# Local-attention scores by 64-column products over both heads, and one 128-column product for a unit's last slot logits

## The chip, the cores and the metric

The program runs on one core of a Trainium2 chip, in one launch. The metric is device time in microseconds, the median of several runs. Engines: TensorE (PE; its weight loads are listed apart as PEld), VectorE (DVE), ScalarE (ACT), GpSimd (POOL) and SyncE (SP), which issues nearly all DMAs here.

## What is computed

An attention layer (batch 4, 8 heads, 576 tokens, head size 64) and two mixture-of-experts layers after it. The change is in the attention's local branch and in the slot logits of the first mixture (a soft one).

```python
q_d, k_d, v_d = (mean over groups of 4 tokens of q, k, v)
out_up = repeat(softmax(q_d @ k_d.T / 8) @ v_d, 4)
mask = abs(pos[:, None] - pos[None, :]) < 4
scores = where(mask, q @ k.T / 8, -1e9)
out_local = softmax(scores) @ v
x = (out_up + out_local)           # (2304, 512) after the heads are joined
logits = x @ phi                   # (2304, 32), 8 experts of 4 slots
d = softmax(logits, axis=0); c = softmax(logits, axis=1)
x = c @ experts(d.T @ x)           # soft mixture
out = top-2 mixture of x           # second mixture, 8 experts
```

## The kernel before

**Units and blocks.** The attention goes over 16 units, each one batch and a pair of heads; the two heads' 64 dimensions fill the 128 partitions. A unit's 576 tokens are cut into 10 groups of 58, each of two halves of 29 (`HQ`); a half needs 35 keys (`KW`). `K` holds the keys [128 dims of both heads, tokens]. `Q` is [128, head, token]: for head h only that head's 64 partitions are filled and the others are zero, so that a product over all 128 partitions gives that head's scores alone.

**Local scores.** `b_s` (line 275) first writes the mask into a PSUM tile by one bf16 product (line 277) and then adds the scores: for 10 groups, 2 halves and 2 heads one product of 32 query columns as weights by 35 keys (line 283), 40 in a unit. Each of the 40 writes 32 of the 128 partitions, in the order half, head, query.

**Soft part and transposes.** `soft_m` to `soft_l2` (lines 295 to 318) make the softmax on DVE and ACT, `soft_p` (line 320) scales the rows on POOL into `P`, and one step later `c_p` (line 361) transposes `P` into `PT`. `d_pe` (line 396) multiplies by the values: 20 products of 64 weight columns by 58 columns of `PT`, each on one quarter of the array (line 405).

**Slot logits.** Two steps later `logit_pe` (line 450) multiplies the unit's output, transposed (`xT`), by `phi_sb`: four products of 32 weight columns by 128 tokens (line 454), and for the last 64 tokens the same product four times, once into each quarter of the partitions (line 457), because `logit_add` (line 461) adds and the slot softmax reads all 128 partitions.

**Order.** The order is written out by hand. In each of the 16 steps a loop (line 577) goes over the table `SEQ` (line 19), and each entry issues one function for the unit of its offset (line 537): `S` is `b_s` of unit p, `CP` and `CD` the transposes of unit p-1, `A0` and `A1` the transposes that bring in keys and queries of unit p+1 (`a_pe`, line 218), `DP` and `DD` the products by values of unit p-1, `EP` and `LG` the transposes and logits of unit p-2. Every engine takes its instructions in that order. After the last step `TSEQ` (line 21) orders the tail.

**Bringing in K and Q.** `a_evac` (line 228) copies the transposed keys and queries out of PSUM, even and odd tokens apart: of a unit's 8 copies ACT makes 6 and DVE 2 (DVE makes the four of `Q` for unit 0). `Q`'s copies write every second element. `a_dve` and `a_pool` (lines 234, 245) sum groups of four tokens on DVE and POOL.

**DMA.** SP issues loads of keys, queries and values for coming units, zero fills of outputs, and the first mixture's weights, in the order of `SEQ`; eight DMAs are in flight at most. When the attention's memory is given back (`ring_2`, line 613) more weights follow. The first mixture, the routing of the second and its expert loop (line 1238 on) come after that.

Of the kernel before, what the change touches and what calls it, by code (L numbers as in the profile page):

```python
# [7 lines left out]
F32 = mybir.dt.float32  # L8
# [4 lines left out]
ALU = mybir.AluOpType  # L13
# [23 lines left out]
def attn_moe_moe_kernel(ctx: ExitStack, tc: tile.TileContext, q, k, v, moe_phi, moe_w1, moe_w2,  # L37
                        w_gate, w_noise, noise, w1, w2, out, dbg=None):
    nc = tc.nc
    B, H, S, D = q.shape  # L40
# [4 lines left out]
    NS = moe_phi.shape[1]  # L45
# [5 lines left out]
    HQ = 29  # L51
    KW = HQ + 6
# [35 lines left out]

    phi_sb = const.tile([128, 4, NS], F32, name="phi_sb")
    wgn = const.tile([128, 4, 2 * E], F32, name="wgn")  # L90
# [17 lines left out]
    with ExitStack() as tctx:  # L108
# [18 lines left out]
        mask = a1.tile([128, NG, KW], BF, name="mask")  # L127
        for a in range(4):
            nc.gpsimd.iota(dk[32 * a:32 * a + 32], pattern=[[1, KW]], base=0, channel_multiplier=-1,
                           allow_small_or_imprecise_dtypes=True)  # L130
        nc.vector.tensor_scalar(mtmp[:, 0], dk, 0.0, -1e9, op0=ALU.is_lt, op1=ALU.mult)
        nc.vector.tensor_scalar(mtmp[:, 1], dk, 6.0, -1e9, op0=ALU.is_gt, op1=ALU.mult)
        nc.vector.tensor_tensor(mtmp[:, 0], mtmp[:, 0], mtmp[:, 1], op=ALU.add)
# [23 lines left out]
        K = a1.tile([128, 592], F32, name="K")  # L157
        Q = a1.tile([128, 2, 592], F32, name="Q")
        Dq = a1.tile([128, 3, 2, 48], F32, name="Dq")
# [6 lines left out]
        for h in range(2):  # L166
            nc.vector.memset(Q[64 * h:64 * h + 64, 1 - h], 0.0)
            nc.vector.memset(Q[64 * h:64 * h + 64, h, S:592], 0.0)

# [58 lines left out]
        def a_evac(u, i, h, r):  # L228
            hs = slice(64 * h, 64 * h + 64)
            dst = Q[hs, h, 0:576] if i else K[hs, 3:579]  # L230
            cp(f"a{i}{h}{r}", dst.rearrange("p (m r) -> p r m", r=2)[:, r], AT[u, i, h][64 * r:64 * r + 64, 0:288],
               u == 0 and i == 1)

        def a_dve(u, h):
            hs = slice(64 * h, 64 * h + 64)
            if h:
                return nc.vector.tensor_reduce(out=Dq[hs, :, h], in_=Q[hs, h, 0:576].rearrange(
                    "p (a n r) -> p a n r", a=3, r=4), axis=AX.X, op=ALU.add)
            q4 = Q[hs, h, 0:576].rearrange("p (n r) -> p n r", r=4)
            q2 = wka.tile([128, 512], F32, name="s2", bufs=1)[hs, 0:288].rearrange("p (n r) -> p n r", r=2)  # L240
            nc.gpsimd.tensor_tensor(q2, q4[:, :, 0:2], q4[:, :, 2:4], op=ALU.add)
            q2 = q2.rearrange("p (a n) r -> p a n r", a=3)
            nc.gpsimd.tensor_tensor(Dq[hs, :, h], q2[:, :, :, 0], q2[:, :, :, 1], op=ALU.add)
# [31 lines left out]
        def b_s(u):  # L275
            s = ps.tile([128, 512], F32, name="S")
            nc.tensor.matmul(s[:, 0:NG * KW], idb, mask.rearrange("p g k -> p (g k)"), start=True, stop=True)
            for g in range(NG):
                for a in range(2):
                    for h in range(2):  # L280
                        p0 = 64 * a + 32 * h
                        c0 = 58 * g + HQ * a
                        nc.tensor.matmul(s[p0:p0 + 32, KW * g:KW * g + KW], Q[:, h, c0:c0 + 32], K[:, c0:c0 + KW],  # L283
                                         start=False, stop=True, skip_group_check=True)
            SS[u] = s
# [110 lines left out]
        def d_pe(u):  # L396
            b, hp = units[u]
            V = Vs[u % 2]
            xl = XL[u]
            PTv = PT.rearrange("p j g (a h i) -> p j g h a i", a=2, h=2)  # L400
            for j in range(5):
                for g in range(2):
                    gs = slice(64 * g, 64 * g + 64)
                    for h in range(2):
                        nc.tensor.matmul(xl[64 * h:64 * h + 64, g, 58 * j:58 * j + 58], V[gs, j, h],  # L405
                                         PTv[gs, j, g, h, :, 0:HQ], start=True, stop=True, skip_group_check=True)
# [43 lines left out]
        def logit_pe(u, t2=None):  # L450
            xT, kk = XT[u], u % 4
            L = (ET_[u][1] if t2 is None else t2)[:, 128:320]
            for t in range(4):
                nc.tensor.matmul(L[32 * t:32 * t + 32, 0:128], phi_sb[:, kk], xT[:, 128 * t:128 * t + 128],
                                 start=True, stop=True, skip_group_check=True)
            for t in range(4):
                nc.tensor.matmul(L[32 * t:32 * t + 32, 128:192], phi_sb[:, kk], xT[:, 512:576], start=True,
                                 stop=True, skip_group_check=True)
            LL[u] = L
# [117 lines left out]
        for p in range(-1, NU - 1):  # L577
            if p == 0:
                nc.sync.dma_start(out=phi_sb, in_=moe_phi.rearrange("(k p) s -> p k s", p=128))
            if p >= 5 and small:  # L580
# [509 lines left out]
    with ExitStack() as gctx:  # L1090
# [94 lines left out]
        for i in range(NTILE - 1):  # L1185
            n = NTILE - 1 - i
# [204 lines left out]
```

## Time and profile before

| | |
|---|---|
| median of 3 runs | 514.81 us (514.27 to 521.28) |
| profiled execution | 511.0 us, of it span 509.2 us |
| attention, from the second unit's step to the last (S of unit 2 to S of unit 15) | 26.7 to 149.2 us of the span |
| first mixture | about 169 to 210 us |
| second mixture | 210 us to the end |
| PE busy | 465.7 us, 91% |
| PE instructions recorded | 5257 products and 5257 weight loads |

Times in the views are microseconds from the start of the span unless marked ns. A 32-bit product is recorded twice (line 283: 640 products in the program, 1280 records), each time with a weight load of its own; a transpose is recorded once. Products are pipelined, so the length of one (some 0.2 us) is much more than the distance to the next. In `128*32 128x35`, 128*32 are the rows and columns of the array that the product takes, and 35 the columns that stream through. "Issue" is idle time in which an engine waited for nothing that the profile shows.

### The profile page before, as it was taken

The page shows a single profiled execution, that of the slowest core. Times are in us where ns is not written, and L with a number is a line of the kernel's source. Part 1 is how long each engine was busy: PE and PEld are TensorE (multiplying, and loading weights), DVE is VectorE, ACT ScalarE, POOL GpSimd, SP SyncE. Part 2 cuts the span into 40 slices and gives each one's busy share as a digit, 9 for nine tenths or more (in the row PEclk, how much of TensorE's full clock was granted, in tenths as well). Part 3 has the DMA queues.
Part 4 walks back from the last instruction along what each step waited for, and adds up shares of the span by engine and source line. Part 5 has one row for each costly group of instructions (what it writes and reads, how often), then busy time and mean ns, then how long its engine had stood idle before and what let it go on. Part 6 is the DMA issues. An engine that isn't in the chain of part 4 may idle for free.

```text
span 509.2 us, 13403 instructions
## 1 busy us (share of the span) xinstructions
PE 465.7 (91%) x5257; PEld 352.8 (69%) x5257; DVE 280.0 (55%) x717; ACT 277.8 (55%) x712; POOL 194.9 (38%) x291
## 2 busy tenths in 40 slices
PE   5798998999798999799969979999999999999993
PEld 4676777767575443477757758788787887878882
DVE  7787888888785321896538226166362552634400
ACT  2778678868676012554238157384662755636410
POOL 5655445535431101076566851232122222222222
PEclk9799899999999999869988989999999999999998
DMA  8999999989957999963373369796856857333333
GB/s 207 280 265 308 256 250 283 244 248 338 262 165 244 397 391 399 396 233 124 118 154 66 65 186 364 207 325 135 237 125 156 265 95 198 41 43 41 41 43 44
DMA packets 74668, 104.90 MB, mean 206 GB/s; under 512 B 30826, under 2 KB 40810, under 8 KB 74602
## 3 DMA queue, kind: packets, MB, share of 16 engines
q1 hardware_dynamic: 67690, 91.15, 55.4%
q0 software_dynamic: 6912, 12.85, 17.1%
q8 instruction: 43, 0.70, 0.6%
q14 instruction: 23, 0.19, 0.1%
HBM read 83.92 MB, written 20.05 MB: 204 GB/s over the span
## 4 chain that ended last, share of the span: by engine, by line
PE 58%; issue 18%; DMA 9%; ACT 5%; DVE 4%; POOL 2%; POOLq 2%; SPq 1%; ACTq 0%
PE y L1044 27%; DMA wr<-in_moe_w_dram 5%; PE S L283 3%; PE xl L412 2%; PE t L224 2%; DMA ld<-in_q_dram 2%; PE Sd L291 2%; PE gx L859 2%; PE hp L785 2%; PE xl L405 2%; PE gx L1024 1%; PE t L366 1%; POOL out_dram L1063 1%; ACT K L212 1%; PE yacc L807 1%
## 5 line engine op out<-in xcount | busy, mean ns | idle before, releaser
L1044 PE MATMUL y<-whi,hl 128*128 128x512 f32 x320 | 129.0, 403 | 0.0
L1044 PE MATMUL y<-whi,hh 128*128 128x512 f32 x320 | 128.6, 402 | 0.3 <-ACT hh L1025 0.3
L1044 PE MATMUL y<-wlo,hh 128*128 128x512 f32 x320 | 128.8, 402 | 0.0
L1063 POOL DMA_INDIRECT out_dram<-ys,idx x40 | 63.4, 1585 | 118.9 <-ACT ys L1050 67.6
L1050 ACT ACTIVATE ys<-y,gt 128x512 f32<-128x512 f32 x40 | 27.5, 687 | 84.5 <-issue 39.9
L1016 DVE TENSOR_TENSOR wlo<-wr,whi 128x512 fp32r<-128x512 f32 x64 | 42.2, 697 | 54.9 <-ACT whi L1013 54.3
L1044 PEld LDWEIGHTS y<-wlo,hh 128*128 128x128 f32 x320 | 61.4, 192 | 14.2 <-issue 1.4
L1044 PEld LDWEIGHTS y<-whi,hl 128*128 128x128 f32 x320 | 61.5, 192 | 11.9 <-issue 2.0
L1044 PEld LDWEIGHTS y<-whi,hh 128*128 128x128 f32 x320 | 61.3, 192 | 12.0 <-ACT hh L1025 0.6
L1026 DVE SCALAR_TENSOR_TENSOR hl<-h,hh 128x256 fp32r<-128x256 f32 (+1 forms) x64 | 31.4, 490 | 32.2 <-ACT hh L1025 30.7
L324 POOL TENSOR_TENSOR P<-El,su 64x350 f32<-64x350 f32 x31 | 24.0, 773 | 65.1 <-DVE su L317 42.8
L988 POOL DMA_INDIRECT tab<-stk,pos x36 | 36.6, 1016 | 16.4 <-issue 15.8
L1025 ACT ACTIVATE hh<-h 128x256 fp32r<-128x256 f32 (+1 forms) x64 | 28.0, 437 | 17.4 <-PE h L1024 12.9
L1013 ACT ACTIVATE whi<-wr 128x512 fp32r<-128x512 f32 x64 | 37.1, 626 | 0.2
L1026 DVE SCALAR_TENSOR_TENSOR hl<-gx,hh 128x256 fp32r<-128x256 f32 (+1 forms) x64 | 31.3, 489 | 9.1 <-ACT hh L1025 7.0
L1025 ACT ACTIVATE hh<-gx 128x256 fp32r<-128x256 f32 (+1 forms) x64 | 28.1, 439 | 14.1 <-PE gx L1024 11.3
L1062 POOL MEMSET spacer<- 1x1 f32 x40 | 18.0, 451 | 39.6 <-issue 39.6
L212 ACT ACTIVATE K<-t 64x288 f32<-64x288 f32 x64 | 27.7, 433 | 5.0 <-PE t L224 3.5
L212 ACT ACTIVATE PT<-t 64x256 f32<-64x256 f32 (+1 forms) x50 | 20.7, 417 | 14.9 <-PE t L366 14.2
L224 PE MATMUL t<-idf,ld 96*128 96x96 f32 x192 | 23.1, 274 | 5.5 <-DMA ld<-in_k_dram 4.3
L224 PEld LDWEIGHTS t<-idf,ld 96*128 96x128 f32 x192 | 19.4, 157 | 9.4 <-DVE on__133 L147 4.3
L875 DVE TENSOR_TENSOR GS<-gx,ghi 32x256 fp32r<-32x256 f32 x28 | 11.7, 419 | 24.1 <-ACT ghi L869 23.6
(297 smaller groups left out, 821.6 us busy)
## 6 DMA issues: line engine op xcount, KB each, us to landing
wr<-in_moe_w_dram SPq DMA_DIRECT2D x120, 256.0 KB
wr<-in_moe_w_dram SPq DMA_DIRECT2D x56, 512.0 KB
out_dram<-zero SPq DMA_DIRECT2D x20, 256.0 KB
V<-in_v_dram SPq DMA_DIRECT2D x62, 80.0 KB
ld<-in_k_dram SPq DMA_DIRECT2D x16, 288.0 KB
ld<-in_q_dram SPq DMA_DIRECT2D x16, 288.0 KB
XT<-tab SPq DMA_DIRECT2D x6, 320.0 KB
tab<-zero SPq DMA_DIRECT2D x7, 256.0 KB
```

The source lines that it names most:

```text
L212: nc.scalar.activation(dst, src, AF.Copy)
L224: nc.tensor.transpose(t[:, c:288:3], ld[:, i, h, 128 * c:128 * c + 128], idf[0:96, 0:96])
L324: eng.tensor_tensor(P[as_, :, HQ * a:HQ * a + KW], El[as_], su[as_, :, None].to_broadcast([64, NG, KW]), op=ALU.mult)
L988: st = nc.gpsimd.indirect_dma_start(out=tab, out_offset=bass.IndirectOffsetOnAxis(ap=pos[:, c, i:i + 1], axis=0), in_=stk[:, i].bitcast(F3 ...
L1013: nc.scalar.activation(whi[:, kk], wb(kk), AF.Copy)
L1016: eng.tensor_tensor(wlo[:, kk], wb(kk), whi[:, kk].bitcast(F32), op=ALU.subtract)
L1025: nc.scalar.activation(hh[:, f], h, AF.Relu)
L1026: nc.vector.scalar_tensor_tensor(hl[:, f], h, 0.0, hh[:, f].bitcast(F32), op0=ALU.max, op1=ALU.subtract)
L1044: nc.tensor.matmul(y, l[:, kk, ts_], r_[:, kk], start=(m == 0), stop=(m == 23))
L1050: nc.scalar.activation(ys, y, AF.Copy, scale=gt[:, ti:ti + 1])
L1062: nc.gpsimd.memset(spacer, 0.0)
L1063: st = nc.gpsimd.indirect_dma_start(out=out, out_offset=bass.IndirectOffsetOnAxis(ap=idx[:, ti:ti + 1], axis=0), in_=ys, in_offset=None, c ...
```

## The change

`Q` becomes [128, token, head]: the two heads' columns of a token stand side by side, so a half's 32 tokens give 64 neighbouring columns, and one product of 64 weight columns writes a half's scores for both heads. The rows of the scores are now ordered half, query, head, and the mask is built for that order (two index fills on POOL in place of four). `d_pe` picks the columns of `PT` accordingly, every second one. The copies out of PSUM into `Q` now write every fourth element (a step of 16 bytes where it was 8). `phi` is kept four times side by side (`phi4`): one is loaded, DVE copies it three times in step 0, and the logits of a unit's last 64 tokens are one product of 128 weight columns.

```diff
-    phi_sb = const.tile([128, 4, NS], F32, name="phi_sb")
+    phi4 = const.tile([128, 4, 4 * NS], F32, name="phi4")
...
-        for a in range(4):
-            nc.gpsimd.iota(dk[32 * a:32 * a + 32], pattern=[[1, KW]], base=0, channel_multiplier=-1,
+        for a in range(2):
+            nc.gpsimd.iota(dk[64 * a:64 * a + 64], pattern=[[2, KW]], base=0, channel_multiplier=-1,
...
-        Q = a1.tile([128, 2, 592], F32, name="Q")
+        Q = a1.tile([128, 592, 2], F32, name="Q")
...
-            dst = Q[hs, h, 0:576] if i else K[hs, 3:579]
+            dst = Q[hs, 0:576, h] if i else K[hs, 3:579]
...
-                    for h in range(2):
-                        p0 = 64 * a + 32 * h
-                        c0 = 58 * g + HQ * a
-                        nc.tensor.matmul(s[p0:p0 + 32, KW * g:KW * g + KW], Q[:, h, c0:c0 + 32], K[:, c0:c0 + KW],
-                                         start=False, stop=True, skip_group_check=True)
+                    c0 = 58 * g + HQ * a
+                    nc.tensor.matmul(s[64 * a:64 * a + 64, KW * g:KW * g + KW],
+                                     Q[:, c0:c0 + 32].rearrange("p i h -> p (i h)"), K[:, c0:c0 + KW],
+                                     start=False, stop=True, skip_group_check=True)
...
-            PTv = PT.rearrange("p j g (a h i) -> p j g h a i", a=2, h=2)
+            PTv = PT.rearrange("p j g (a i h) -> p j g h a i", a=2, h=2)
...
-                nc.tensor.matmul(L[32 * t:32 * t + 32, 0:128], phi_sb[:, kk], xT[:, 128 * t:128 * t + 128],
+                nc.tensor.matmul(L[32 * t:32 * t + 32, 0:128], phi4[:, kk, 0:NS], xT[:, 128 * t:128 * t + 128],
                                  start=True, stop=True, skip_group_check=True)
-            for t in range(4):
-                nc.tensor.matmul(L[32 * t:32 * t + 32, 128:192], phi_sb[:, kk], xT[:, 512:576], start=True,
-                                 stop=True, skip_group_check=True)
+            nc.tensor.matmul(L[:, 128:192], phi4[:, kk], xT[:, 512:576], start=True, stop=True, skip_group_check=True)
...
-                nc.sync.dma_start(out=phi_sb, in_=moe_phi.rearrange("(k p) s -> p k s", p=128))
+                nc.sync.dma_start(out=phi4[:, :, 0:NS], in_=moe_phi.rearrange("(k p) s -> p k s", p=128))
+                nc.vector.tensor_copy(phi4[:, :, NS:4 * NS].rearrange("p k (t s) -> p k t s", t=3),
+                                      phi4[:, :, None, 0:NS].to_broadcast([128, 4, 3, NS]))
```

On PE, from the logits of one unit to the scores of the next, this stands before (each row: line, operation, written and read tiles, rows and columns written, how many):

```order
L432 MATMUL t<-idf,xT 128x128 x4
L434 MATMUL t<-idf,xT 64x128
L454 MATMUL t<-xT,phi_sb 32x128 x4
L457 MATMUL t<-xT,phi_sb 32x64 x4
L412 MATMUL xl<-PdT,Vd 64x144 x4
L277 LDWEIGHTS idb
L277 MATMUL S<-mask,idb 128x350
L283 MATMUL S<-K,Q 32x35 x40
```

And this, at the same place, with the change (lines have moved up by one to three; `phi_79` is `phi4`):

```order
L431 MATMUL t<-idf,xT 128x128 x4
L433 MATMUL t<-idf,xT 64x128
L453 MATMUL t<-xT,phi_79 32x128 x4
L455 MATMUL t<-xT,phi_79 128x64
L411 MATMUL xl<-PdT,Vd 64x144 x4
L277 LDWEIGHTS idb
L277 MATMUL S<-mask,idb 128x350
L281 MATMUL S<-K,Q 64x35 x20
```

Nothing changes its place on PE: 40 products became 20 of twice the columns, and four became one.

On DVE, at the start of step 0, the difference is one added copy, ahead of the first unit's softmax:

```order
+L599 MEMSET P 128x640
+L577 COPY phi_79<-phi_79 128x4x96
+L297 TENSOR_REDUCE m<-S 128x10
+L304 TENSOR_TENSOR El<-S,m 128x350
+L329 TENSOR_REDUCE md<-Sd 96x3
```

The copy stands between the clearing of `P` and the row maximum of unit 0, so whatever it waits for, the first softmax waits for too.

## Rows read from the trace of the kernel before

**Rows 1.** The page: busy time of each engine, and granted PE clock in 40 slices.

```profile
PE 465.7 (91%) x5257; PEld 352.8 (69%) x5257; DVE 280.0 (55%) x717; ACT 277.8 (55%) x712; POOL 194.9 (38%) x291
...
PEclk9799899999999999869988989999999999999998
```

**Rows 2.** Busy time by stage: stretch, length, engines (and records), clock, DMA share, GB/s.

```profile
26.70:149.20 122.50, 111.29 (x2649) 86.54 (x2648) 97.98 (x256) 93.95 (x293) 59.93 (x92) 0.99 0.93 267
82.00:90.00 8.00, 7.73 (x200) 6.33 (x199) 6.72 (x17) 7.01 (x22) 3.60 (x6) 1.00 0.98 285
...
96.20:100.10 3.90, 3.57 (x127) 2.55 (x127) 3.06 (x10) 2.97 (x13) 2.93 (x6) 1.00 0.81 155
...
72.99:79.92 6.93, 5.51 (x124) 4.88 (x124) 5.67 (x16) 5.24 (x14) 1.82 (x4) 1.00 1.03 274
...
169.00:210.00 41.00, 40.18 (x551) 16.97 (x552) 11.94 (x51) 9.91 (x26) 3.95 (x10) 1.00 1.04 394
```

**Rows 3.** Waits from 26 to 149 us: who for whom, us, times, longest.

```profile
PE xl L405 <- issue: 3.4, 3, 1.5
...
PEld t L224 <- ACT PT L212: 2.9, 12, 0.5
PE S L283 <- issue: 2.6, 5, 1.2
...
PE Sd L291 <- issue: 1.4, 1, 1.4
PEld t L432 <- issue: 1.4, 1, 1.4
...
PE t L457 <- issue: 0.9, 1, 0.9
...
PE t L224 <- DMA ld<-in_q_dram: 0.8, 1, 0.8
```

**Rows 4.** The page: the DMA queue that carries PE's instructions (packets, MB, share).

```profile
q8 instruction: 43, 0.70, 0.6%
```

**Rows 5.** PE in order of time, quiet step: start, length, records.

```profile
82.08 0.91 PE L283 MATMUL S<-K,Q 128*32 128x35 f32 x80
...
87.07 0.81 PE L405 MATMUL xl<-PT,V 64*64 64x58 f32 x40
87.81 0.66 PE L432 MATMUL t<-idf,xT 128*128 128x128 f32 x4
...
88.52 0.43 PE L454 MATMUL t<-xT,phi_sb 128*32 128x128 f32 x8
88.77 0.29 PE L457 MATMUL t<-xT,phi_sb 128*32 128x64 f32 x8
88.99 0.86 PE L412 MATMUL xl<-PdT,Vd 128*64 128x144 f32 x8
```

**Rows 6.** Groups by line, 26 to 150 us, PE: busy us, mean ns of one.

```profile
L283 PE MATMUL S<-K,Q 128*32 128x35 f32 x1120 | 14.6, 202 | 2.6 <-issue 2.6
...
L405 PE MATMUL xl<-PT,V 64*64 64x58 f32 x520 | 11.4, 223 | 3.4 <-issue 3.4
```

**Rows 7.** The chain that ended last: a stall; eight records of 128 weight columns by 32.

```profile
48.97 1.54 issue
...
167.54 0.89 PE t L654 x8
```

**Rows 8.** DVE in order of time at the start.

```profile
10.48 0.52 DVE L298 TENSOR_REDUCE m<-S 128x10 f32<-128x350 f32 x1
```

**Rows 9.** Groups by line, 26 to 150 us, ACT: copies into Q and into PT.

```profile
L212 ACT ACTIVATE Q<-t 64x288 f32<-64x288 f32 x26 | 11.1, 428 | 1.0 <-PE t L224 0.2
...
L212 ACT ACTIVATE PT<-t 64x256 f32<-64x256 f32 x26 | 9.9, 379 | 0.6
```

**Rows 10.** ACT in order of time, quiet step: the last copy into K.

```profile
88.27 0.43 ACT L212 ACTIVATE K<-t 64x288 f32<-64x288 f32 x1
```

**Rows 11.** POOL in order of time, quiet step: its first sum over K.

```profile
88.84 0.67 POOL L249 TENSOR_TENSOR s<-K 128x288 f32<-128x288 f32 x1
```

More of the change, by code (lines that the diff above doesn't have):

```diff
@@ L127, in attn_moe_moe_kernel @@
         mask = a1.tile([128, NG, KW], BF, name="mask")
-        for a in range(4):
-            nc.gpsimd.iota(dk[32 * a:32 * a + 32], pattern=[[1, KW]], base=0, channel_multiplier=-1,
+        for a in range(2):
+            nc.gpsimd.iota(dk[64 * a:64 * a + 64], pattern=[[2, KW]], base=0, channel_multiplier=-1,
                            allow_small_or_imprecise_dtypes=True)
-        nc.vector.tensor_scalar(mtmp[:, 0], dk, 0.0, -1e9, op0=ALU.is_lt, op1=ALU.mult)
-        nc.vector.tensor_scalar(mtmp[:, 1], dk, 6.0, -1e9, op0=ALU.is_gt, op1=ALU.mult)
+        nc.vector.tensor_scalar(mtmp[:, 0], dk, -1.5, -1e9, op0=ALU.is_lt, op1=ALU.mult)
+        nc.vector.tensor_scalar(mtmp[:, 1], dk, 12.5, -1e9, op0=ALU.is_gt, op1=ALU.mult)
         nc.vector.tensor_tensor(mtmp[:, 0], mtmp[:, 0], mtmp[:, 1], op=ALU.add)
@@ L166, in attn_moe_moe_kernel @@
         for h in range(2):
-            nc.vector.memset(Q[64 * h:64 * h + 64, 1 - h], 0.0)
-            nc.vector.memset(Q[64 * h:64 * h + 64, h, S:592], 0.0)
+            nc.vector.memset(Q[64 * h:64 * h + 64, :, 1 - h], 0.0)
+            nc.vector.memset(Q[64 * h:64 * h + 64, S:592, h], 0.0)
         def tp():
@@ L236, in a_dve @@
             if h:
-                return nc.vector.tensor_reduce(out=Dq[hs, :, h], in_=Q[hs, h, 0:576].rearrange(
+                return nc.vector.tensor_reduce(out=Dq[hs, :, h], in_=Q[hs, 0:576, h].rearrange(
                     "p (a n r) -> p a n r", a=3, r=4), axis=AX.X, op=ALU.add)
-            q4 = Q[hs, h, 0:576].rearrange("p (n r) -> p n r", r=4)
+            q4 = Q[hs, 0:576, h].rearrange("p (n r) -> p n r", r=4)
             q2 = wka.tile([128, 512], F32, name="s2", bufs=1)[hs, 0:288].rearrange("p (n r) -> p n r", r=2)
```

## The prediction

> **What bounds the kernel now.** I read the page first: PE is busy 91% of the span, DVE and ACT 55% [rows 1]. Then the stages. From the second unit's scores to the last unit's, 122.5 us hold 111.3 us of PE work, and all other engines are further from full [rows 2]; the 11.2 us in which PE idles there are the place to look. The list of waits says what they are: 3.4 + 2.6 + 1.4 + 1.4 + 0.9 = 9.7 us in 11 stalls are "issue", with nothing waited for, and 0.8 us is one late load of queries [rows 3]. A step without a stall (82 to 90 us) has PE busy 7.73 of 8.00 us and ACT 7.01 [rows 2]. So in the attention PE's own sequence sets the pace, and a nanosecond added to it counts once per unit.
>
> **What the stalls are.** The queue of PE's instructions moved 0.70 MB in 43 packets [rows 4], 16.3 KB each; PE has 2 x 5257 records [rows 1], 245 for each packet. From the end of the stall before 96.2 us to the end of the next at 100.1 there are 127 + 127 = 254 records, and from 72.99 to 79.92, again between two ends of stalls, 248 [rows 2]. So a stall stands where one packet's instructions are used up and the next packet is not there. These two blocks took 3.9 and 6.9 us, stall included: that is how long a packet can take while the data queues are full (DMA share 0.81 and 1.03 there). [...]
>
> **The scores: dearer on PE.** Before, a unit's 80 records run four at a time, each on 32 of the array's 128 columns: (0.91 - 0.202) us / 79 = 9.0 ns from one to the next [rows 5, 6], 36 ns on one tile of the array. After, 40 records of 64 weight columns run two at a time, so the same 20 stand on each tile, and the question is how long one takes there. Two rows bear on it. The products by values have 64 weight columns too, on four tiles: (0.81 - 0.223) / 39 = 15.1 ns, 60 ns on a tile [rows 5, 6]. And eight records of 128 weight columns by only 32 streaming columns took 0.89 us, 111 ns each [rows 7]: there the weight load, 0.87 ns a column, sets the distance, since the stream is a quarter of it. By that, 64 weight columns take 56 ns, whatever the 35 columns that stream need. I take 58 ns: 20 x (58 - 36) = 0.44 us more in a unit, 16 x 0.44 = +7.0 us. Ends: if the records kept today's 9.0 ns, 40 of them would save 0.35 us a unit (-5.6 us); if the loads of the two tiles could not overlap, 40 x 58 = 2.3 us instead of 0.7 would cost 1.6 us a unit (+26 us). The nearest row, line 405, overlaps on four tiles, so I keep 58.
>
> **The last 64 tokens' logits: also dearer.** What goes is the stretch from the first record of line 457 to the next line: 88.99 - 88.77 = 0.22 us [rows 5]. What comes is one product, two records, of 128 weight columns: 2 x 111 = 0.22 us [rows 7], and it takes the whole array between a product on quarters and one on halves. Such a change of shape costs a pause: the last record of line 405 started at 87.07 + 0.81 - 0.223 = 87.66, the next line at 87.81 [rows 5, 6], 0.15 us, of which some 0.05 us is its own stream. One more such pause is added (0.10), and the last stream of 64 columns with the pause behind it (0.15) was there before and is part of the 0.22 that goes; so 0.10 + 0.22 + 0.15 - 0.22 = +0.25 us, 16 x 0.25 = +4.0 us. Ends: 0 (pause and loads overlap) to +0.4 a unit (two pauses of 0.15 in full), 0 to +6.4 us.
>
> **The stalls: cheaper.** A stall costs its idle time and the overlap of one record, 0.2 us: 9.7 + 11 x 0.2 = 11.9 us. A quiet step has 200 + 199 records [rows 2]. The scores lose 40 products' records and 40 loads, the logits 6 and 6: 399 - 92 = 307. A block of 254 records took 254/399 x 8.0 = 5.1 us of a quiet step; it will take 254/307 x (8.0 + 0.44 + 0.25) = 7.2 us. That is more than both blocks above took with their stalls, so most packets will be in time, and there are 307/399 = 0.77 as many. I leave 2.6 us for late ones, in the denser parts of a step or in steps with slot work: -9.3 us. Ends: -11.9 (none left) to -2.7 (each block stalls as before, only their number falls).
>
> **Smaller terms.** [...] The transposes of line 224 wait 2.9 us in 12 steps for ACT to empty their buffers [rows 3]; when the scores are longer, DVE and ACT, which finish the unit before, are less late, and I let half go, -1.4 us (0 to -2.9). The added copy of phi stands ahead of DVE's first row maximum at 10.48 us, an operation of 350 columns that takes 0.52 [rows 8]; the copy has 384, so 0.57 at most unless its load is late, and ACT and PE have some slack there: +0.3 once (0 to 2). Reading PT at every second element is taken as free, since line 405 is bound by its weights by the same argument; +0.4 us a unit if the stream doubled. The copies into Q at a coarser step I take as free too: ACT has 1 us a step to spare [rows 2] and PE is getting longer. If PE should run ahead, the late load of queries (0.8 us) grows and takes back up to 2 us; at equal pace, 0. After the attention nothing changes by itself: the weights of the first mixture start when the attention gives its memory back, and from 169 to 210 us DMA is full at 394 GB/s [rows 2], so what the attention's end moves, the end moves.
>
> **Sum:** 7.0 + 4.0 - 9.3 - 1.0 - 1.4 + 0.3 = -0.4 us, with rounding and nothing for the load -0.5, on a profiled execution of 511.0 us. The median of the runs shown is 514.8 us; the same difference puts it at 514.3 us.
>
> **Rivals.** (1) Weights are not the bound on two tiles: the loads of 64 columns hide, the scores stay at 36 ns a tile and cost nothing more. For it: half of the array's columns are free of the other tile's loads. Against it: 111 ns in rows 7. Then 514.3 - 7.0 = 507.3 us. (2) Slower: the stalls stay. A packet's arrival is set by the full data queues (share 0.93 over the attention [rows 2]), not by how fast PE eats; each block loses what it lost, and only 0.77 of them are left: 9.2 us instead of 2.6, so 514.3 + 6.6 = 520.9 us. For it: one block took 6.9 us with its stall, near the 7.2 that I give the new ones. Against it: the other took 3.9. It decides as soon as more than 3.1 us of stalls remain; from there on the two dearer products win. (3) The copies into Q become slow. They write every fourth element, 16 bytes apart. Today's step of 8 bytes costs little: 428 ns for 288 elements against 379 for 256 into a plain row [rows 9], which in proportion are 426 for 288. If the step of 16 bytes doubles them, ACT does 2 x 0.43 us more in a step, its last copy into K ends later by that, and POOL, which starts on K 0.14 us after that copy [rows 10, 11], is late with what the next step needs; 0.86 - 0.14 = 0.72 against the 0.69 by which PE's step grows leaves next to nothing each step, and unit 0, whose four copies DVE makes one after another, loses 4 x 0.43: 514.3 + 1.7 + 0.5 = 516.5 us. [...]
>
> **How the numbers follow.** Forecast (weights bind, most stalls go) 0.52, alone 510 to 518 us; rival 1 0.14; rival 2 0.22; rival 3 0.12. The cases lie at 507, 514, 516.5 and 521, so most of the chance is within 1.5% of today. The range of 505 to 522 us holds rival 1 with 2 us to spare and rival 2 with 1; the outer ends (-5.6 and +26 us for the scores) fall outside, with some 0.15. Two per cent, about what a measurement of this kernel can tell from no change, is 10.3 us. Faster than 504.5 us needs rival 1 and no stall left at all: 0.07. Slower than 525.1 us needs rival 2 together with rival 3, or loads that don't overlap: 0.07. Within: 0.86.
>
> **What would show it.** Right: the group of 40 records in the scores about 1.3 us long in place of 0.91; a line of two records behind the logits, 0.1 us apart or more; "issue" on PE from 26 to 149 us down from 9.7 to some 2 us; the instruction queue with some 6 packets less; steps without a stall of 8.5 to 8.7 us. Wrong: scores of 0.9 us or less (rival 1), five or more stalls of a microsecond (rival 2), copies into Q above 0.5 us (rival 3), or the attention's end moved by more than 8 us either way.

## The result and the profile after

The changed kernel took 516.71 us (median of 17 runs), the kernel before 514.18 us (17 runs beside them). The ratio of the runs is 1.0075, with a 95% interval of 1.0050 to 1.0101: some 3.9 us slower (2.6 to 5.2), within two per cent, but not by chance. The forecast had been 0.5 us faster. The time lies inside the range given, the direction was wrong. Slow runs are left out of this ratio and of those below (so 1.0075 is not 516.71/514.18 = 1.0049), and the profile of run 14 is of a slow run, so that its stretch, stalls and clock say nothing here.

The page, the row over the attention, and the waits of PE (26 to 149 us), all of the changed kernel:

```profile
PE 471.4 (92%) x4521; PEld 356.6 (69%) x4521; DVE 292.3 (57%) x718; ACT 284.9 (55%) x712; POOL 198.4 (39%) x289
...
q8 instruction: 38, 0.62, 0.5%
```

```profile
26.70:149.20 122.50, 116.60 (x2034) 90.48 (x2031) 106.48 (x252) 100.60 (x293) 63.22 (x91) 1.00 0.90 266
```

```profile
PEld t L433 <- ACT Q L212: 8.2, 10, 0.9
...
PE t L433 <- ACT Q L212: 5.8, 10, 0.6
...
PEld t L224 <- ACT PT L212: 2.7, 12, 0.2
```

Against [rows 1 to 4]: PE has 736 records less, the instruction queue five packets less (q14, the page's other instruction queue, moved 23 in both), and the clock over the attention is 1.00 (0.99 before). PE's "issue" stalls are gone altogether (9.7 us in 11 before; the rows of "issue" that are left are weight loads of 0.2 us and three of 0.8 in slot work, the extra products that come once in a batch). In the kernel before each of the 11 ends 1.2 to 1.7 us after a packet of 16 KB on q8 has landed (one starts at 47.94 us and takes 0.92, and PE goes on at 50.52), so they are called fetch stalls below. In their place stands a wait that was small in the kernel before: in ten steps, all but those with slot work, line 433 (the transpose of the last 64 tokens) waits some 0.6 us for ACT's copy into Q. The prediction did not have it.

PE in a step without a stall, in order of time (start, length, records):

```profile
84.22 1.36 PE L281 MATMUL S<-K,Q 128*64 128x35 f32 x40
...
90.16 0.66 PE L431 MATMUL t<-idf,xT 128*128 128x128 f32 x4
91.40 0.30 PE L433 MATMUL t<-idf,xT 128*64 128x128 f32 x1 [0.58 <-ACT Q L212]
91.62 0.42 PE L453 MATMUL t<-xT,phi 128*32 128x128 f32 x8
91.98 0.43 PE L455 MATMUL t<-xT,phi 128*128 128x64 f32 x2
92.34 0.86 PE L411 MATMUL xl<-PdT,Vd 128*64 128x144 f32 x8
```

Against [rows 5]: the scores take 1.36 us (0.91). From the start of line 453 over the last tokens' logits (line 455) to the next line it is 92.34 - 91.62 = 0.72 us (88.99 - 88.52 = 0.47), 0.25 more. And between the starts of lines 431 and 433 lie 1.24 us, where before it was 0.49 (87.81 to 88.30). ACT in the same step, and below it three rows of the kernel before that belong beside it (from the step of [rows 5], ACT's copies into Q and PE's transpose of the last 64 tokens; from the waits of 26 to 149 us, that transpose's weight load):

```profile
86.16 1.29 ACT L212 ACTIVATE PT<-t 64x384 f32<-64x384 f32 x3 [1.21 <-PE t L365]
87.47 0.69 ACT L212 ACTIVATE PdT<-t 128x288 f32<-128x288 f32 x2
88.07 0.48 ACT L309 ACTIVATE El<-El 128x350 f32<-128x350 f32 x1
88.57 1.35 ACT L212 ACTIVATE K<-t 64x288 f32<-64x288 f32 x3
89.95 1.39 ACT L212 ACTIVATE Q<-t 64x288 f32<-64x288 f32 x2
91.37 0.43 ACT L212 ACTIVATE K<-t 64x288 f32<-64x288 f32 x1
```

```profile
87.35 0.89 ACT L212 ACTIVATE Q<-t 64x288 f32<-64x288 f32 x2
```

```profile
88.30 0.29 PE L434 MATMUL t<-idf,xT 128*64 128x128 f32 x1
```

```profile
PEld t L434 <- ACT Q L212: 1.3, 4, 0.3
```

ACT waits 1.21 us for PE's transposes of P, then works without a pause for 5.2 us up to the end of the second copy into Q at 91.34; 0.06 us later PE writes line 433's buffer, which is the one that this copy empties. PE then goes through logits, line 411, mask, scores to the next transposes of P, for which ACT waits. That is a closed loop: each engine waits for the other once in a step. Before, in the step of [rows 5], Q's copies ended at 88.24 and that transpose began at 88.30, the same 0.06 us behind: nothing was to spare. And in four other steps its weight load stood idle for 0.3 us until that copy was done. The two of them without a stall took 8.08 and 8.10 us, the step of [rows 5], which follows a stall, 7.96. So the loop was closed before the change, and a row of its list of waits said so; the step is called 8.0 us below.

The groups of lines that changed, 26 to 150 us; first of the changed kernel, then of the kernel before (ACT's 428 ns for Q is in [rows 9]):

```profile
L212 ACT ACTIVATE Q<-t 64x288 f32<-64x288 f32 x27 | 18.6, 689 | 1.4 <-PE t L224 0.8
...
L214 DVE COPY Q<-t 64x288 f32<-64x288 f32 x26 | 17.6, 677 | 0.6
...
L241 POOL TENSOR_TENSOR s<-Q 64x288 f32<-64x288 f32 x13 | 12.2, 942 | 1.0
```

```profile
L214 DVE COPY Q<-t 64x288 f32<-64x288 f32 x26 | 11.9, 457 | 0.9 <-PE t L224 0.4
...
L241 POOL TENSOR_TENSOR s<-Q 64x288 f32<-64x288 f32 x14 | 9.3, 661 | 1.1
```

The copies into Q at 16 bytes cost 61% more on ACT and 48% more on DVE, POOL's sum that reads Q 43% more; in a step ACT has 2 x 0.26 = 0.52 us more to do, all of it in the loop.

The sum over the attention: from the third unit's scores (26.45 before, 27.25 after) to the last unit's (148.93, 151.20) 122.5 us became 123.9. Thirteen steps without a stall went from 8.0 to 9.15 us, +15.0. What lies above that pace went from 122.5 - 13 x 8.0 = 18.5 us to 123.9 - 13 x 9.15 = 5.0, so -13.5: the stalls, what followed them, and the waits they caused (the slot work is in both; 0.05 us on the step before would be 0.65 us here). With 0.8 us more in front and 0.8 behind, the attention's last product (lines 654 and 653) starts at 170.45 in place of 167.38, 3.1 us later. The two profiled executions differ by 5.7 us; the other 2.6 fall behind the attention, where no line was changed. That part took between 339 and 345 us in all the runs profiled for this study, so a single execution of it proves nothing at this size.

### The profile page after: what moved, and what is told of

It is laid out like the page before. It is cut to its first block, busy times and chain, and to the rows that moved or that the text cites. A ratio compares the mean times of both kernels' runs of the same rounds, so it can differ in the third digit from the quotient of the medians.

```text
span 514.9 us, 11931 instructions
## 1 busy us (share of the span) xinstructions
PE 471.4 (92%) x4521; PEld 356.6 (69%) x4521; DVE 292.3 (57%) x718; ACT 284.9 (55%) x712; POOL 198.4 (39%) x289
## 4 chain that ended last, share of the span: by engine, by line
PE 48%; issue 12%; DMA 12%; ACT 11%; POOL 10%; DVE 2%; POOLq 2%; SPq 1%; ACTq 0%
PE y L1043 25%; DMA wr<-in_moe_w_dram 7%; POOL tab L987 5%; PE S L281 4%; ACT Q L212 3%; ACT K L212 3%; ACT PT L212 2%; POOL out_dram L1062 2%; PE xl L411 2%; DMA out_dram<-ys,idx 2%; PE gx L858 2%; PE t L365 2%; DMA w10b<-in_moe_w_dram 2%; POOLq L1068 1%; PE Sd L290 1%
## 5 line engine op out<-in xcount | busy, mean ns | idle before, releaser
L1024 ACT ACTIVATE hh<-gx 128x256 fp32r<-128x256 f32 (+1 forms) x64 | 28.1, 439 | 13.5 <-PE gx L1023 11.3
L281 PE MATMUL S<-K,Q 128*64 128x35 f32 x640 | 23.8, 235 | 5.1 <-DVE Q L214 2.7
L1023 PE MATMUL h<-XS,GS 128*128 128x256 f32 (+1 forms) x64 | 21.1, 329 | 7.1 <-DVE hl L1025 7.1
L281 PEld LDWEIGHTS S<-K,Q 128*64 128x64 f32 x640 | 21.9, 149 | 8.1 <-POOL s L241 3.2
```

Of the source, the lines that this page charges most:

```text
L281: nc.tensor.matmul(s[64 * a:64 * a + 64, KW * g:KW * g + KW], Q[:, c0:c0 + 32].rearrange("p i h -> p (i h)"), K[:, c0:c0 + KW], start=Fals ...
L1023: nc.tensor.matmul(h, GS[:, 128 * f:128 * f + 128], XS[e][:, c0:c0 + n], start=True, stop=True)
L1024: nc.scalar.activation(hh[:, f], h, AF.Relu)
```

## The experiments

Theory 1: the step is the loop through PE and ACT. Theory 2: PE's sequence alone sets the pace. In the table, "step" is the distance of two starts of the mask's product in the timeline, in steps without a stall or slot work; "stretch" is that from the third unit's to the last's; "issue" is what PE's rows of that name add up to from 26 to 149 us (for the kernel before without the one stall, 1.4 us, that stands on a weight load); "clock" is the granted one there. These four come from one profiled execution of each kernel. The ratio is to the kernel before, run beside it.

| kernel | step, us | stretch, us | issue, us | clock | ratio (95%) |
|---|---|---|---|---|---|
| before | 8.0 to 8.1 | 122.5 | 8.3 | 0.99 | 1 |
| changed | 9.15 | 123.9 | 0 | 1.00 | 1.0075 (1.0050 to 1.0101) |
| 1 cheap copies | 8.64 | 118.5 | 0 | 1.00 | 1.0014 (0.996 to 1.007) |
| 2 P's transposes first | 9.10 | 122.5 | 0 | 1.00 | 1.0065 (1.002 to 1.011) |
| 3 before, logits alone | 8.2 | 120.6 | 4.2 | 0.99 | 1.0012 (0.997 to 1.005) |
| 4 before, slow copies alone | 8.66 | 123.3 | 5.1 | 0.99 | 1.0052 (1.000 to 1.010) |
| 5 K before Q | 8.39 | 124.6 | 3.6 | 0.99 | 1.0146 (1.007 to 1.022) |
| 6 before, K before Q | 7.92 | 128.3 | 12.1 | 0.93 | 1.0009 (0.997 to 1.005) |
| 7 logits as before | 8.91 | 122.8 | 1.1 | 0.99 | 1.0057 (1.002 to 1.010) |
| 8 5 and 7 | 8.35 | 122.6 | 3.3 | 0.97 | 0.998 (0.993 to 1.003) |
| 9 dummy products | 9.2 | 136.2 | 3.7 | 0.94 | 1.020 (1.013 to 1.027) |
| 10 1 and 5 | 8.39 | 121.4 | 2.4 | 0.99 | 1.0033 (0.997 to 1.009) |
| 11 K copy on DVE | 9.17 | 126.7 | 0 | 0.97 | 1.0142 (1.010 to 1.018) |
| 12 11 and 7 | 9.18 | 126.2 | 0 | 0.97 | 1.0144 (1.009 to 1.020) |
| 13 other K copy on DVE, Vd first | 8.6 to 9.2 | 125.1 | 1.9 | 0.99 | 1.0121 (1.006 to 1.018) |
| 14 other K copy on DVE | 8.9 | 127.6 | 3.1 | 0.96 | 1.0010 (0.996 to 1.006) |

### 1. The changed kernel with cheap copies

```diff
-            dst = Q[hs, 0:576, h] if i else K[hs, 3:579]
+            dst = Q.rearrange("p n h -> p (h n)")[hs, 592 * h:592 * h + 576] if i else K[hs, 3:579]
... (Q is cleared whole at the start)
```

> The changed kernel, but the copies into Q write at a step of 8 bytes as before the change (each head's queries in a row of its own of the same tile; the 64 weight columns of a score are then not the queries that belong to it, and what follows from the scores is computed from other numbers). Theory 1 (the pace of a step is a loop through two engines: PE from the second transpose of L433 over logits, L411, mask and scores to the transposes of P, then ACT from the copies of PT over PdT, El and K to the copies into Q, whose end releases L433 again): two copies of ACT in the loop get about 0.26 us shorter each, so the step goes from 9.15 to about 8.63 us, 13 to 14 steps give -7, and the four slow copies of DVE in the first unit about -0.9: 507 to 511 us, faster than before the change too. Theory 2 (PE's own sequence sets the pace, the copies lie beside it, and the 0.9 us a step lost are the dearer scores and logits): the wait before L433 shrinks and turns up elsewhere, 515 to 517 us.

The copies took 428 ns again and the step 8.64 us; theory 1 had said 8.63. The stretch is 118.5 us, 5.4 below the changed kernel and 4.0 below the kernel before. So 0.52 us a step of the loss are the copies, one to one, and theory 2 is out. (DVE's two copies into Q got cheap with ACT's; run 5 below keeps both dear and has a shorter step, so it is not DVE's that set it.) The whole kernel gained less than forecast (513.24 us, no measurable difference from 511.92 before, and the interval touches that of the changed kernel, so that a gain of the whole is not shown): in the profiled execution the clock fell from 163 us on, at the attention's end, which it did not in either of the two kernels compared. PE by stretch (length, busy, clock, DMA share, GB/s):

```profile
162.00:164.00 2.00, 2.00 (x22) 0.75 0.95 315
164.00:168.00 4.00, 4.00 (x21) 0.50 1.03 410
168.00:170.00 2.00, 2.00 (x21) 0.54 0.89 361
```

By these granted clocks 2 x 0.25 + 4 x 0.50 + 2 x 0.46 = 3.4 us of work are lost.

### 2. The changed kernel with P's transposes ahead of the scores

```diff
-SEQ = """S SK CP EP01 ...
+SEQ = """CP S SK EP01 ...
```

> The changed kernel, with the transposes of P (L365) ahead of the mask and the scores in the order of a step, on PE and nothing else. Theory 1: the mask and the scores (1.54 us from L277 to L365) leave the loop and lie beside ACT's copies; the loop alone would need 9.15 - 1.54 = 7.6 us, PE's own work (8.3 us a step without its wait) takes over, so 8.3 to 8.5 us a step, -9 to -11 us, 505 to 508 us if the fetch stalls stay away; up to 515 if all of them (9.7 us before) come back. PE's wait at L433 goes from 0.84 us to under 0.2. Theory 2 (PE's own sequence sets the pace): an order of the same instructions on PE is worth nothing, 515 to 517 us, and the wait at L433 only moves.

Theory 1 failed here: 9.10 us a step, and the wait at L433 as long as in the changed kernel. Theory 2 had the time (515 to 517 us, measured 515.26) but a wait that moves, and run 1 had ruled it out. ACT in order of time shows what held the step:

```profile
84.62 1.29 ACT L212 ACTIVATE PT<-t 64x384 f32<-64x384 f32 x3
87.08 0.69 ACT L212 ACTIVATE PdT<-t 128x288 f32<-128x288 f32 x2 [1.16 <-PE t L376]
```

The PT copies did move ahead (they start 6.4 us before line 433, 5.2 in the changed kernel); then ACT stood for the transposes of Ed (L376), which come on PE behind scores and Sd. In the changed kernel that path ends within 0.1 us of the one over P. The loop has two legs (ways from PE to ACT) of one length, over P and over Ed, and theory 1 had named only one.

### 3 and 4. The kernel before with one half of the change each

```diff
# 3 (with phi4 as in the change)
...
-                nc.tensor.matmul(L[32 * t:32 * t + 32, 128:192], phi_sb[:, kk], xT[:, 512:576], start=True,
+            nc.tensor.matmul(L[:, 128:192], phi4[:, kk], xT[:, 512:576], start=True, stop=True, skip_group_check=True)
# 4
...
-        Q = a1.tile([128, 2, 592], F32, name="Q")
+        Q = a1.tile([128, 592, 2], F32, name="Q")
-                        nc.tensor.matmul(s[p0:p0 + 32, KW * g:KW * g + KW], Q[:, h, c0:c0 + 32], K[:, c0:c0 + KW],
+                        nc.tensor.matmul(s[p0:p0 + 32, KW * g:KW * g + KW], Q[:, c0:c0 + 32, h], K[:, c0:c0 + KW],
... (the other places that write or read Q likewise)
```

> The kernel before, with the change of the last 64 tokens' logits alone (phi four times side by side, one product of 128 columns in place of four of 32). Both theories: +0.20 to +0.25 us a step by PE, 16 units, so +3 to +4 us, less what 12 records fewer a unit take off the fetch stalls (192 records of some 250 to a packet: about one stall, -0.9): +1 to +4 us, 515 to 518 us. What it settles is whether the stalls stay (8 to 10 us of them) when the records of the scores stay.

> The kernel before, with the layout of Q by (token, head) alone: the 20 blocks are scored as before by 80 products per unit... that is 40 products of 32 columns of each head, now taken at a step of 8 bytes, and the copies into Q write at 16 bytes. Theory 1: ACT's two copies in the loop get 0.26 us longer each, so a step without a fetch stall goes from 8.0 to 8.5 us; part of the stalls that lie beside ACT's part of the loop are covered then: +3 to +8 us, 517 to 522 us. Theory 2 (copies beside PE's sequence): 0 to +2 us, 514 to 516.

(The second text counts the 80 records of the 40 products as products at one place.) The logits alone: 8.2 us a step, 0.1 to 0.2 more, with half of the stalls (4.2 us) and no measurable difference for the whole, where 1 to 4 us more were expected. The slow copies alone: 8.66 us a step, 0.6 more where theory 1 had 0.5, and the same long wait:

```profile
PEld t L434 <- ACT Q L212: 7.2, 9, 0.9
...
PE t L434 <- ACT Q L212: 5.1, 9, 0.6
```

So the layout of Q alone makes the loop the pace, with the old scores. The stretch got only 0.8 us longer; the ratio of 1.0052 just reaches 1, and the median of 515.05 us lies where theory 2 had it, not at theory 1's 517 to 522.

### 5 and 6. The fourth K copy ahead of the Q copies

```diff
-... a001 W a000 SU SU_ A1 a010 P1 a100 a101
-a110 a111 a011 P0 ...
+... a001 W a000 SU SU_ A1 a010 P1 a011 a100 a101
+a110 a111 P0 ...
```

> The changed kernel, with ACT's fourth copy into K (a011) ahead of its two copies into Q in the order of a step; nothing else moves on PE. The second transpose of the last 64 tokens (L433) then takes the PSUM buffer of K's second head, free after the fourth K copy. Theory 1, as the two runs with cheap copies and with P's transposes first leave it (the step is a loop: L433, logits, L411, scores, Sd, the transposes of Ed and P, then on ACT from the PdT or PT copies to the copy that frees L433's buffer; 8.65 us with cheap copies, 9.11 with P's transposes first because the path over Ed is as long): the release comes about 1.0 us earlier (two Q copies of 0.69 less one K copy of 0.43), the loop alone would be 8.2, PE's own work (8.3 us a step) takes over: 8.3 to 8.5 us a step, -9 to -11 us in the attention against the changed kernel, PE's wait at L433 under 0.2 us. Rival (the wait at L433 is a symptom, another chain, over POOL's P, s and Ed or over DVE, holds the step at 9.1): 9.0 to 9.15 us a step, and the wait turns up in another place.

> The kernel before with the same edit (fourth K copy ahead of the two Q copies). Theory 1: the loop was the pace there too (8.0 us in a step without a fetch stall), the release comes 0.4 to 0.9 us earlier, PE's own work of some 7.6 to 7.7 us a step takes over, the fetch stalls stay (9 to 10 us): quiet steps 7.6 to 7.8 us, -3 to -5 us in the attention. Rival: quiet steps stay at 8.0, nothing changes.

In the changed kernel the step fell from 9.15 to 8.39 us, as theory 1 said. PE, then ACT, in order of time:

```profile
87.86 0.66 PE L431 MATMUL t<-idf,xT 128*128 128x128 f32 x4
88.35 0.27 PE L433 MATMUL t<-idf,xT 128*64 128x128 f32 x1
```

```profile
86.27 1.81 ACT L212 ACTIVATE K<-t 64x288 f32<-64x288 f32 x4
88.11 1.43 ACT L212 ACTIVATE Q<-t 64x288 f32<-64x288 f32 x2
```

Line 433 starts 0.49 us behind line 431, with no wait. But the stretch is no shorter (124.6 us) and the kernel slower (520.72 us). What came back, PE's waits from 26 to 149 us:

```profile
PE xl L411 <- issue: 3.0, 1, 3.0
...
PE t L224 <- DMA ld<-in_k_dram: 1.7, 1, 1.7
...
PE S L281 <- issue: 0.6, 2, 0.4
PE t L224 <- DMA ld<-in_q_dram: 0.6, 1, 0.6
```

In the kernel before, the same edit gave little: steps of 7.91 and 7.94 us where 8.08 and 8.10 had been, between theory 1 (7.6 to 7.8) and the rival (8.0). The wait of line 434 is gone, and what is left is PE's own pace, higher than theory 1 had taken it. But fetch stalls rose to 12.1 us, the clock fell to 0.93, and the whole is no faster.

### 7 and 8. The logits as before; and with K before Q

```diff
-            nc.tensor.matmul(L[:, 128:192], phi4[:, kk], xT[:, 512:576], start=True, stop=True, skip_group_check=True)
+            for t in range(4):
+                nc.tensor.matmul(L[32 * t:32 * t + 32, 128:192], phi4[:, kk, 0:NS], xT[:, 512:576], start=True,
+                                 stop=True, skip_group_check=True)
```

> The changed kernel with the last 64 tokens' logits by four products of 32 columns, as before the change (weights from phi's first copy). Theory 1: logits lie in the loop between L433 and the scores, so the step is shorter by the 0.20 to 0.25 us they got dearer: 8.90 to 8.95 us a step instead of 9.15, -3 us in the attention; 12 records more a unit bring back at most one or two fetch stalls, as the wait at L433 is left. Rival (fetch stalls come with the count of records alone): four or five stalls of 0.8 us come back, no gain.

> Both edits on the changed kernel: fourth K copy ahead of the Q copies, and the logits as before the change; what is left of the change is the merged scores and the dear copies. Theory 1: PE's own work sets the step, 8.3 less 0.2 to 0.25 us, 8.05 to 8.3 us a step; -12 to -14 us in the attention against the changed kernel if the stalls stay away, -5 if they come back; against the kernel before -4 to -10. Rival (another chain holds the step at 9.1): 8.9 to 9.1 us a step.

The first: 8.91 us a step, 0.24 less, so the logits too count one to one; two stalls came back (1.1 us). The second: 8.35 us a step, only 0.04 less than run 5, and outside the 8.05 to 8.3 expected: in each step without slot work the weight load of line 411 now stands idle 0.3 us until DVE's copy Vd is done, which takes back most of what the logits give. Stalls of 3.3 us and a clock of 0.97 come to it, and so 122.6 us for the stretch and the time of the kernel before (0.998). That is the lowest ratio of the kernels that hold the merged scores, and no gain.

### 9 and 10. PE's wait filled, and PE's wait taken away

```diff
# 9, in e_pe between the two groups of transposes
...
+                for n in range(20):
+                    nc.tensor.matmul(SX[u + 2][32 * (n % 4):32 * (n % 4) + 32, 400:435], idf[:, 0:32], idf[:, 0:35],
+                                     start=True, stop=True, skip_group_check=True)
```

> The changed kernel with 20 products more in each unit, of the form of the scores before the change (32 weight columns, 35 columns of output, into unused columns of S, read by nobody), between the first and the second group of transposes of the last tokens, where PE waits 0.6 to 0.8 us for Q's copy on ACT. PE's count of records in a step is then that of the kernel before less 12. Theory 1 (the loop through ACT is the pace): 0.46 us of work in a wait of 0.6 to 0.8 costs nothing, steps of 9.15 us stay. On the fetch stalls: theory A (they come with the number of records in a step, whatever PE waits for) expects 4 to 8 us of them back in the attention; theory B (the changed kernel hides its fetches in the wait at L433 and in steps that are longer) expects 0 to 2 us of them. Rival to theory 1 (PE's work sets the pace): 9.6 us a step, +6 us.

> The run with the copies into Q at 8 bytes (queries then not those of their heads, as told there) with the fourth K copy ahead of the two Q copies as well. Theory 1: the release of L433's buffer is then 0.4 us earlier still than 8.65 us a step allows, PE's own work is the pace: 8.3 to 8.4 us a step, as with K first and dear copies (8.39), so that the dear copies are worth nothing any more. Rival (PE gets quicker with ACT's copies, there is a third chain): under 8.2, or 8.6 as before. On the fetch stalls: theory A expects none, as in all three runs so far that have this code for PE and a wait; theory B expects 2 to 5 us of them, as there is no wait left (3.9 us with K first and dear copies).

With dummies a step without a stall takes 9.21 to 9.29 us: 20 products that need some 0.46 us of PE (an estimate, half of the 0.91 us that 40 of this form take in [rows 5]) cost 0.1, theory 1 again. Yet the stretch is 12.2 us longer. Stalls of 3.7 us came back, just under what theory A had and over theory B, and the clock fell to 0.50 twice, for some 7 us each time. PE by stretch, around the second:

```profile
136.00:138.50 2.50, 1.06 (x42) 1.00 0.33 66
138.50:140.70 2.20, 1.83 (x22) 0.84 0.90 251
140.70:142.00 1.30, 1.30 (x11) 0.50 1.08 377
142.00:145.00 3.00, 3.00 (x45) 0.50 0.99 327
```

Cheap copies with K first: 8.39 us a step, the same as with dear copies. PE's own pace is thus 8.39 us, and with the loop open the copies' price no longer matters. Stalls: 2.4 us where theory A expected none. Neither theory of the stalls is right alone. By the table: 306 records a step and a wait of PE in most steps (changed, 1, 2, 11): no stall. The same records and no wait (5, 10): 2.4 to 3.6 us. 398 records and a wait of 0.6 us (4): 5.1; 398 and at most a wait of 0.3 us of a weight load (before, 6): 8.3 to 12.1. Both seem to count, and the wait at L433 would then have hidden in the changed kernel what fewer records alone would not have hidden. That is argued and not shown: each figure is one execution, and other runs do not fall in line. Run 1 has no stall with a wait as short as that of the kernel before, while 318 records and waits give 1.1 (7), 3.3 (8) and none (12).

### 11 to 14. A K copy from ACT to DVE

```diff
# 11 (12: with the logits as before)
-ON_V = ['a110', 'a111', 'k0', 'p00', 'v0', 'v1']
+ON_V = ['a000', 'a110', 'a111', 'k0', 'p00', 'v0', 'v1']
# 13 and 14
+ON_V = ['a010', 'a110', 'a111', 'k0', 'p00', 'v0', 'v1']
-... a001 W a000 SU SU_ A1 a010 P1 a100 a101
+... a001 W a000 a010 SU SU_ A1 P1 a100 a101
# 13 alone
-a110 a111 a011 P0 KD DQ0 VD z DP V0 V1 DQ1 ...
+a011 P0 KD DQ0 VD z DP V0 V1 a110 a111 DQ1 ...
```

> The changed kernel with one of ACT's three copies into K that stand in the loop (a000) given to DVE; nothing is left out. Theory 1 (loop through PE and ACT): the loop gets 0.43 us shorter, 8.7 us a step instead of 9.15, and PE still waits 0.3 to 0.4 us a step at L433, so that the fetch stalls stay away as in the run with cheap copies (8.65 us a step, no stall): -5 to -6 us in the attention against the changed kernel, about 118.5 us from the third unit's scores to the last's. For the whole kernel 510 to 514 us; up to 3 us of it can be lost again to the clock behind the attention, as in the two runs that were through with it before 147 us. Rival (DVE, busy 106 of 122 us, becomes the pace): 8.9 to 9.2 us a step, no gain.

> The run before this one with the last 64 tokens' logits as before the change as well. Theory 1: 8.7 less 0.23 us, 8.45 to 8.55 us a step, near PE's own pace of 8.35, so with little wait left and 12 records more a unit, and some 2 to 5 us of fetch stalls with a fall of the clock behind one or two of them: the attention as long as without this edit or 1 to 2 us shorter, 509 to 514 us. Rival (DVE is the pace): 8.9 us a step as with the logits alone.

Theory 1's forecasts were both wrong: 9.17 us, where its rival (DVE is the pace) had it, and 9.18, above even that rival's 8.9. PE, then DVE, of the first in order of time:

```profile
86.12 0.86 PE L411 MATMUL xl<-PdT,Vd 128*64 128x144 f32 x8 [0.39 <-DVE Vd L214]
```

```profile
82.82 0.45 DVE L214 COPY K<-t 64x288 f32<-64x288 f32 x1 [0.69 <-ACT K L212]
```

DVE's copy waits for ACT's copy into the same rows of K, so DVE's later Vd is late for line 411, and a leg through DVE takes over at the old length. That the logits then no longer matter (9.17 and 9.18) says the same.

> The changed kernel with ACT's third copy into K (a010, the second head's rows, so that it waits for no copy of ACT) given to DVE ahead of the sums of the softmax, and DVE's two Vd copies ahead of its two Q copies; nothing is left out. Theory 1 with both legs shorter: ACT's leg loses 0.43 us, 8.70 to 8.75 us a step, PE waits at L433 for Q by 0.3 us still, no wait at L411 for Vd, no or one fetch stall: from the third unit's scores to the last's 118 to 120 us, the kernel 510 to 514 us. Rival (DVE, with 8.4 us of work a step and its own waits, is the pace): 9.0 us a step or more.

> The same without the Vd copies moved. Theory 1 (two legs): ACT's leg is 8.7, but Vd comes 0.3 to 0.45 us later on DVE while PE would reach L411 0.45 us earlier: a wait of 0.1 to 0.4 us at L411 for Vd, 8.8 to 9.0 us a step. Rival (DVE is the pace as a whole): the same as the run with Vd first, within 0.05 us a step.

With the copy that waits for nobody, steps are 8.9 us without Vd moved (in most of them a wait of 0.1 to 0.4 us at L411, as theory 1 had it) and 8.6 to 9.2 with it, where a wait at L411 is left only once, at the start. So the wait goes where theory 1 sent it, but the step does not: the median is 8.92 us in both, not 8.70 to 8.75 in run 13, and two runs alike is what the rival had. DVE is busy 9.28 of 10 us in run 13 (82 to 92 us), so whether it holds the step as a whole stays open. The stretch of run 13 got no shorter than 125.1 us, by a stall of 1.9 us, the clock and the slot steps. No version here beats the kernel before.

## Why the prediction was wrong

**Scores, right.** The group is 1.36 us long (about 1.3 forecast); its 40 records have 1.14 us between the first and the last start, 58 ns on each tile, the value taken from the 111 ns of [rows 7]. Rival 1 is out.

**Logits, right.** +0.25 a unit forecast; the rows above give 0.25 on PE, runs 3 and 7 0.1 to 0.2 and 0.24 us a step.

**Stalls, right for an incomplete reason.** Forecast: 2.6 us left; measured: none. That stalls fall to the packets that still come late was half of it (the 11 stalls of the kernel before do end behind a landed packet, as shown above). In runs 5 and 10, with the same instructions and no wait of PE, 2.4 to 3.6 us are left, which is about the number forecast. That the rest was hidden by the wait that the prediction had not seen is the likely reading, not a shown one.

**The clock, right in direction.** The sum takes 1.0 us off for a fall of the clock that goes; no run shows that term. What the runs show is one fall in the attention of the kernel before, to a granted clock of 0.50 with 1.7 us of work lost, and none in that of the changed kernel.

**The copies into Q, wrong; this is the step that failed.** "The copies into Q at a coarser step I take as free too: ACT has 1 us a step to spare [rows 2] and PE is getting longer." Each half was true by the rows, the conclusion was not. ACT's spare microsecond is one wait, at the transposes of P, and PE's release at line 433 comes from ACT's copy 5.2 us later. The two engines' added times are not side by side but one behind the other in the loop, so they add: 8.0 + 0.52 (run 1) + 0.24 (run 7) = 8.76, and the remaining 0.39 up to 9.15 is the scores' 0.44, as near as the 8.0 is known (7.96 to 8.10). The sign was on record: the wait of line 434's weight load for ACT's copy into Q, 0.3 us in four steps, stands in the list of waits from which [rows 3] were taken. "In the attention PE's own sequence sets the pace" was thus not quite true before the change either: run 6 has 7.91 and 7.94 us for PE alone where the kernel before took 8.08 and 8.10. The forecast had 8.5 to 8.7 us, PE alone; runs 5 and 10 show 8.39 for PE alone, since PE's wait of 0.27 us for line 224 goes too (7.73 us of work in [rows 2] and 0.44 + 0.25 make 8.42). The loop costs 9.15 - 8.39 = 0.76 us a step, 9.9 us over 13 steps.

**Why the miss is only some 4 us.** PE's own growth, less line 224's waits, had been entered with 11.0 - 1.4 = 9.6 us, and at 8.39 us a step it is 16 x 0.39 = 6.2; what goes with the stalls and the clock had been entered with 9.3 + 1.0 = 10.3 us, and 13.5 went. The two take back 6.6 of the 9.9 us that were missing. That the time fell into the range is this luck, and not the sum.

**Rival 3 had the right mechanism at too low a price.** It saw slow copies and K's last copy, and compared ACT's 0.72 us with PE's 0.69 as if one could cover the other. The doubling that it supposed for the copies is shown by no run: they went from 428 to 689 ns on ACT and from 457 to 677 on DVE. Its 516.5 us is near the measured time by luck: its working has almost nothing in the steps, where run 1 finds 0.52 us in each.

**"What the attention's end moves, the end moves" is not shown.** Run 1 came to the last unit's scores 4.0 us before the kernel before and lost that in the profiled execution by the falling clock and the later part; the part behind the attention varies by more than what was to be carried over.

## What to carry to other kernels

An engine's spare time is worth what its last wait allows: before an instruction on it is called free, follow its result to the next wait of the engine that sets the pace, buffers included, and see whether that one comes back to it within the step. Here the release already came no earlier than it was needed, and the row of four waits of 0.3 us was the sign of it: a short wait of the engine that sets the pace can tell more than a microsecond of idle time on the other. Then a faster step is not yet a faster kernel: taking the wait away (8.39 us in place of 9.15) brought back fetch stalls (3.6 us in run 5), late loads (2.3) and a lower clock (0.99 for 1.00), and the sum was no better.

## What was not expected of the hardware

More work can be lost behind a pause of PE than the pause is long. In the kernel before, behind the fetch stall of 1.54 us in [rows 7], by stretch (length, busy, clock, DMA share, GB/s):

```profile
48.90:50.50 1.60, 0.07 (x6) 1.00 1.21 219
50.50:52.00 1.50, 1.48 (x27) 0.90 1.14 208
52.00:55.00 3.00, 3.00 (x85) 0.50 1.04 316
55.00:58.00 3.00, 3.00 (x59) 0.98 0.85 256
```

The granted clock falls to 0.50 (52 to 55 us) shortly after PE works again at 50.52, and 1.5 x 0.10 + 3 x 0.50 + 3 x 0.02 = 1.7 us of work are lost. Run 6 (mean clock 0.93 over 123 us, 8.6 us lost) and run 9 (0.94) show what several of them do. It need not be a fetch stall: in run 11, which has none, PE waits 1.9 us for Vd up to 27 us, and the clock is at 0.50 from 28 to 34. The changed kernel, with a wait of 0.6 us of its matmuls in most steps and no fetch stall, has no fall in the attention (1.00). Not every stall is followed by a fall (one fall behind 11 stalls in the kernel before), and what decides was not tried.

A copy from PSUM that writes every fourth word (16 bytes) takes 689 ns on ACT for 288 words in each of 64 partitions, and 428 ns for every second word; on DVE 677 and 457. DVE's sum over four neighbours that reads Q at 8 in place of 4 bytes took 752 and 750 ns, no difference.
